# Retention kernel: first tables and products reordered at the head (broadcast table loads, a second DMA queue, twelve zero products)

## The chip, the cores and the metric

The kernel runs on one core of a Trainium2 chip, as one program and one launch. The metric is the device time of that core in microseconds, lower is better. The kernel before took 921.67 us (median of 3 runs, 921.03 to 922.06).

## The reference

Three layers follow one another. The first is a retention (attention with a decaying state) over 4 batches, 8 heads, 768 tokens, head size 64. The second and third are dense layers over the 3072 tokens.

```
state = gamma * state + k_t (outer) v_t          # per head, gamma = 1 - 2^(-5-h)
y_t   = (1/8) * q_t @ state
x     = y as (3072, 512)
h     = x @ w_in                                 # 512 -> 2048
g     = h if h >= 1, 0 if h <= -1, (h+1)^2/4 between
x     = g @ w_out                                # 2048 -> 512
then: softmax-gated layer of 1024, layer norm, times g_ln, @ w2_out
```

## The kernel before, in words

The retention is cut into 24 units: 4 batches of 6 chunks of 128 tokens. One unit `attention(u, env)` is a Python generator; it takes its queries and keys as a tile `qk` and its keys and values as a tile `kv` (512 KB each). The steps of a unit are these:

- Load `qk` (L183) and `kv` (L186) through SyncE's DMA queue, called SP below. Two yields follow.
- Scores `qp` on TensorE (L206): 8 products of 64 rows, two heads to each of four pairs.
- On VectorE `qn` = queries times the table `qdec` (L209, not for the first chunk of a batch). On GpSimd (POOL in the profile) keys times `vdec` (L211). On VectorE `sm` = scores times the table `dmat` (L215), once for each of the two head parities `o`. A yield follows.
- On TensorE `pv` = state times `qn` (L264, not for the first chunk) plus values times `sm` (L268), and `sp` = keys (decayed) times values (L273), which is what the chunk adds to the state.
- The result is split into a high and a low part (L104 on ScalarE, called ACT below, and L105 on VectorE, called DVE). The state is decayed (L280) and added to (L284, L286).

The tables are made by `tables()` (L298 to L309), called once after the first attention slot: `vdec` is loaded (L299), then `dmat` by four loads of 64 partitions each (L302), `gdec` (L303) and `qdec` (L304). Then for each `o` VectorE multiplies `dmat` by `vdec` (L306) and GpSimd sets what lies above the diagonal to zero (L307). GpSimd multiplies `qdec` by `gdec` (L309). In the source table of `dmat` the rows 0 to 63 are equal among each other, and so are the rows 64 to 127.

The order of work is set by a dictionary `sched` of slots: a unit is advanced by one yield in each of four slots. Unit 0 is advanced in the slots -11, -6, -5 and -4, unit 1 one slot later each, and so on. Weights of the second layer are loaded 512 KB at a time through the same SP queue (`load_w`, L113) seven or eight slots ahead and converted on ScalarE and VectorE (`conv_w`, L122 to L133). The first conversion step is the ACT instruction of L122. Within one engine the framework's planner orders the instructions by priority in a simulated timeline, then the order is fixed. `in_row()` adds dependencies that keep TensorE's instructions of a group in the order in which they were written.

At the start 40 products of zeros (`wps`, L413, 128x128 bf16) run on TensorE while the first loads are on their way. The dense layers (L363, L391, L493, L545) follow from about 45 us on.

Of the kernel before, what the change touches and what calls it, by code (L numbers as in the profile page):

```python
# [9 lines left out]
F32 = mybir.dt.float32  # L10
# [12 lines left out]
C = 128  # L23
NCH = S // C
NU = B * NCH
NPAIR = H // 2
# [12 lines left out]
ROW = CPB  # L39
W0 = -4  # L40
WARM = 40
PER = 4
GB = 3
HP_ATT = 1000
# [6 lines left out]
def kernel(  # L51
# [15 lines left out]
    nc = tc.nc  # L67
    ve, sc, gp, pe = nc.vector, nc.scalar, nc.gpsimd, nc.tensor
# [6 lines left out]
    ps_h = ctx.enter_context(tc.tile_pool(name="ps_h", bufs=2, space=bass.MemoryType.PSUM))  # L75
# [6 lines left out]
    vdec = const.tile([128, H, 1], F32, tag="vdec", name="vdec")  # L82
    gdec = const.tile([128, NPAIR, 1], F32, tag="gdec", name="gdec")
# [6 lines left out]
    @contextmanager  # L90
    def in_row():

        done, last = {i.name for i in nc.cur_bb.bb.instructions}, None
        yield
        for i in nc.cur_bb.bb.instructions:
            if i.name in done or i.engine != mybir.EngineType.PE:
                continue
            if last is not None:
                tc.add_manual_dep(i, last.name, mybir.DependencyInfo(
                    mybir.DependencyClass.NoSync, mybir.DependencyReason.DATA), reason="in a row")  # L100
            last = i
# [9 lines left out]
    def load_w(src, pool=wp):  # L111
        raw = pool.tile([128, 512, 2], U32, tag="w", name="w_raw")
        state["last_w"] = nc.sync.dma_start(raw.rearrange("p a t -> p (a t)"), src.bitcast(U32))  # L113
        return raw

    def conv_w(raw, scale=None):
        lw, hw = raw[:, :, 0], raw[:, :, 1]
        m = cv.tile([128, 512], F32, tag="wm", name="wm", bufs=3)
        p = cv.tile([128, 512], F32, tag="wp", name="wp", bufs=2)
        mu, mi = m.bitcast(U32), m.bitcast(I32)  # L120

        sc.activation(m, hw.bitcast(F32), AF.Abs)  # L122
        ve.tensor_scalar(m, m, W_MIN, W_MAX, op0=ALU.max, op1=ALU.min)

        sc.activation(p, lw, AF.Copy, bias=2.0, scale=2.0 ** -51)
        ve.tensor_scalar(mu, mu, 3, None, op0=ALU.logical_shift_left)
        ve.scalar_tensor_tensor(mu, hw, 0x80000000, mu, op0=ALU.bitwise_and, op1=ALU.bitwise_xor)  # L127
        ve.tensor_tensor(out=mi, in0=mi, in1=p.bitcast(I32), op=ALU.add)
        w = wp.tile([128, 2, 512], F32R, tag="w", name="w")
        hi, lo = w[:, 0, :], w[:, 1, :]  # L130
        if scale is None:
            sc.activation(hi, m, AF.Copy)
            ve.tensor_tensor(out=lo, in0=m, in1=fl(hi), op=ALU.subtract)  # L133
        else:
            sc.activation(hi, m, AF.Copy, scale=scale)
            ve.scalar_tensor_tensor(lo, m, scale, fl(hi), op0=ALU.mult, op1=ALU.subtract)
        return hi, lo
# [11 lines left out]
    def load_swapped(dst, src):  # L149
        n = NPAIR // 2  # L150
        ax = (slice(None),) * (len(dst.shape) - 3)
        nc.sync.dma_start(dst[(slice(None), *ax, slice(0, n))], src[(slice(None), *ax, slice(0, n))])
        for h in range(2):
            nc.sync.dma_start(dst[(slice(64 * h, 64 * h + 64), *ax, slice(n, 2 * n))],
                              src[(slice(64 - 64 * h, 128 - 64 * h), *ax, slice(n, 2 * n))])

    def attention(u, env):
# [4 lines left out]
        if blk == 0:  # L162
            def banks(*names):
                return [ps_acc.tile([128, 512], F32, tag="acc", name=n) for n in names]
# [16 lines left out]
        with (ExitStack() if early else tc.issue_after(state["last_w"].ins)):  # L181
            if not quad:
                nc.sync.dma_start(qk, qk_t[b, c])  # L183
            else:
                load_swapped(qk, qk_t[b, c])
            nc.sync.dma_start(kv, kv_t[b, c])  # L186
        yield
        yield
# [10 lines left out]
                sc.activation(env["dmat"][r][:, :2], dmat[:, r, :2], AF.Copy)  # L199
                sc.activation(env["dmat"][r][:, 2:], dmat[:, 1 - r, 2:], AF.Copy)  # L200
        qp = [t.rearrange("a (p c) -> a p c", p=NPAIR) for t in banks("qp0", "qp1")]
        with (in_row() if u >= ROW else ExitStack()):
            for p in range(NPAIR):
                for o in range(2):
                    r = slice(64 * o, 64 * o + 64)
                    pe.matmul(qp[o][:, p, :], qk[r, 1, p, :], qk[r, 0, p, :], start=True, stop=True)  # L206
        if not first:
            qn = attp.tile([128, NPAIR, C], F32, tag="qn", name="qn", bufs=1)
            ve.tensor_tensor(out=qn, in0=qk[:, 0], in1=env["qdec"], op=ALU.mult)  # L209
# [13 lines left out]
        if quad:  # L223
# [3 lines left out]
            with (in_row() if u >= ROW else ExitStack()):  # L227
                if not first:
                    for j in range(2):
                        for g in range(2):  # L230
                            for r in range(2):
                                o = r ^ g
                                pe.matmul(pv[r][64 * o:64 * o + 64, j, :], st[64 * r:64 * r + 64, 2 * g + j, :D],  # L233
                                          qn[64 * r:64 * r + 64, 2 * g + j, :], start=(j == 0), stop=False, skip_group_check=True)
                for r in (1, 0):
                    for j in range(2):
                        for o in range(2):
                            p = 2 * (r ^ o) + j
                            pe.matmul(pv[r][64 * o:64 * o + 64, j, :], kv[:, 1, 2 * p + o, :], sm[r][:, p, :],  # L239
                                      start=(first and j == 0), stop=(j == 1), skip_group_check=True)  # L240
                if not last:
                    for p in range(NPAIR):
                        for r in range(2):
                            h = 2 * p + (r ^ (p // 2))
                            pe.matmul(sp[64 * r:64 * r + 64, p, :], kv[:, 0, h, :], kv[:, 1, h, :],  # L245
                                      start=True, stop=True, skip_group_check=True)
# [14 lines left out]
        with (in_row() if u >= ROW else ExitStack()):  # L261
            if not first:
                for p in range(NPAIR):
                    pe.matmul(pv[:, p, :], st[:, p, :], qn[:, p, :],  # L264
                              start=(p == 0), stop=False, skip_group_check=True)
            for p in range(NPAIR):
                for o in range(2):
                    pe.matmul(pv[64 * o:64 * o + 64, p, :], kv[:, 1, 2 * p + o, :], sm[o][:, p, :],  # L268
                              start=(first and p == 0), stop=(p == NPAIR - 1), skip_group_check=True)
            if not last:  # L270
                for p in range(NPAIR):
                    for o in range(2):
                        pe.matmul(sp[64 * o:64 * o + 64, p, :], kv[:, 0, 2 * p + o, :], kv[:, 1, 2 * p + o, :],  # L273
                                  start=True, stop=True)
# [20 lines left out]
    dmat = attp.tile([128, 2, NPAIR, C], F32, tag="dmat", name="dmat", bufs=1)  # L295
    qdec = attp.tile([128, NPAIR, C], F32, tag="qdec", name="qdec", bufs=1)

    def tables():  # L298
        nc.sync.dma_start(vdec, vdec_d)  # L299
        for o in range(2):  # L300
            for dup in range(2):
                nc.sync.dma_start(dmat[64 * dup:64 * dup + 64, o], xtab_d[64 * o:64 * o + 64])  # L302
        nc.sync.dma_start(gdec, gdec_d)  # L303
        nc.sync.dma_start(qdec, xtab_d)  # L304
        for o in range(2):
            ve.tensor_tensor(out=dmat[:, o], in0=dmat[:, o], in1=vdec[:, o::2].to_broadcast([128, NPAIR, C]), op=ALU.mult)  # L306
            gp.affine_select(out=dmat[:, o], in_=dmat[:, o], pattern=[[0, NPAIR], [1, C]], compare_op=ALU.is_ge,  # L307
                             fill=0.0, base=0, channel_multiplier=-1)
        gp.tensor_tensor(out=qdec, in0=qdec, in1=gdec.to_broadcast([128, NPAIR, C]), op=ALU.mult)  # L309
# [17 lines left out]
    for u in range(NU):  # L327
        blk, k = divmod(u, CPB)
        x = (k - CPB, SA - CPB + k)[blk] if blk < 2 else base[blk] - NF + PER * k + 2
        at = (x - STEP0, x - 2, x - 1, x) if u < NWP else (x - 6, x - 3, x - 2, x)  # L330
        for n in at:
            sched.setdefault(n, []).append(u)
    gens = {}

    def att_slot(s):
        for u in sched.get(s, []):
            if u not in gens:
                gens[u] = attention(u, env)
            with (tc.high_priority(offset=HP_ATT) if u >= NWP else ExitStack()):
                next(gens[u], None)  # L340
# [3 lines left out]
    def weights_slot(s):  # L344
        for f in range(NF):
            at = max(first_use[f], W0 + 2 * f)
            if s == at - LD - 1:
                wraw[f] = [load_w(w_in[f])]
            if s == at - LD:
                wraw[f].append(load_w(w_out[f]))  # L350
            if s == at - CL:
                wi[f] = conv_w(wraw[f][0])
            if s == at - CL + 1:
                wo[f] = conv_w(wraw[f][1])
# [52 lines left out]

    if WARM:
        wz = const.tile([128, 128], mybir.dt.bfloat16, tag="wz", name="wz")
        ve.memset(wz, 0.0)  # L410
        wps = ps_h.tile([128, 512], F32, tag="h", name="wps")
        for n in range(WARM):
            pe.matmul(wps[:, :128], wz, wz, start=(n == 0), stop=(n == WARM - 1))  # L413
    for s in range(min(min(sched), -LD - 1), 0):
        att_slot(s)
        if s == min(sched):
            tables()
        weights_slot(s)

    w2 = [(w2_in[k, n], (k, n), w2i, None) for k in range(KD) for n in range(2)] + \  # L420
# [38 lines left out]
    if True:  # L459
# [94 lines left out]
        for t in range(NTILE + 3):  # L554
            if t % TPB == 0 and t // TPB + 1 < NBLK:
                load_x2(t // TPB + 1)
            for st in steps:
                n = int(st[-1]) if st[-1] in "01" and st[:2] in ("tr", "ou") else 2 if st == "out2" else 0
# [68 lines left out]
```

## Time and profile before

| what | value |
|---|---|
| median of 3 runs | 921.67 us (921.03 to 922.06) |
| the profiled execution | 921.52 us, its span on the core 919.7 us |
| TensorE busy | 902.7 us (98% of the span) |
| VectorE busy | 581.2 us (63%) |
| ScalarE busy | 406.2 us (44%) |
| GpSimd busy | 29.0 us (3%) |
| mean granted TensorE clock | 0.998 of full speed |
| moved by DMA | 75.35 MB, mean 82 GB/s |

The span goes from the first to the last instruction, and the execution's own time is 1.8 us longer. In the profile PE is TensorE, PEld its weight loads, DVE VectorE, ACT ScalarE, POOL GpSimd and SP SyncE. Times are in microseconds from the start of the span.

### The profile page before, as it was taken

What the parts mean: (1) busy time and instruction counts of PE and PEld (TensorE: products, weight loads), DVE (VectorE), ACT (ScalarE), POOL (GpSimd) and SP (SyncE); (2) the same over time, 40 slices, a digit from 0 to 9 for tenths busy, and PEclk for the clock granted to TensorE, in tenths of its full rate; (3) what the DMA queues carried; (4) which work ended last, traced back from release to release, by engine and by line L of the source; (5) the groups of instructions that cost most, each with busy time, mean ns of one, the idle gap of its engine ahead of it and who ended that gap; (6) DMA issues with size and microseconds to landing.
All of it is one profiled execution on the core that took longest, in us unless ns stands there. A gap on an engine that the chain in (4) does not pass through costs nothing.

```text
span 919.7 us, 12967 instructions
## 1 busy us (share of the span) xinstructions
PE 902.7 (98%) x5016; PEld 742.3 (81%) x5016; DVE 581.2 (63%) x1358; ACT 406.2 (44%) x765; POOL 29.0 (3%) x29
## 2 busy tenths in 40 slices
PE   8899999999999999999999999999999999999998
PEld 7678888887778887888888888888888888888886
DVE  5999997234354334332445449823988888888885
ACT  3768876333243444343445448732333333333322
POOL 3100100000010000000000000000000000000000
PEclk9999999999999999999999999999999999999999
DMA  9940821004431202220204114301111010100000
GB/s 338 407 160 24 321 70 58 1 23 138 126 127 47 69 24 93 69 62 8 75 18 148 59 37 148 118 0 47 47 60 43 29 63 24 69 24 24 24 24 34
DMA packets 30604, 75.35 MB, mean 82 GB/s; under 512 B 3920, under 2 KB 10448, under 8 KB 29776
## 3 DMA queue, kind: packets, MB, share of 16 engines
q1 hardware_dynamic: 29392, 72.44, 22.0%
q10 hardware_dynamic: 1152, 2.10, 1.0%
q8 instruction: 39, 0.64, 0.3%
q14 instruction: 21, 0.17, 0.1%
HBM read 59.85 MB, written 14.68 MB: 81 GB/s over the span
## 4 chain that ended last, share of the span: by engine, by line
PE 93%; DVE 2%; DMA 2%; ACT 1%; issue 0%; SPq 0%; ACTq 0%; DVEq 0%
PE acc L391 28%; PE hp L363 27%; PE h2p L493 14%; PE op L545 14%; PE tp L534 2%; PE pa L206 2%; PE pa L239 1%; DMA xs<-x2p 1%; PE pa L268 1%; PE pa L233 1%; PE qp L206 1%; PE pv L268 1%; PE pa L264 1%; DMA x2d<-xs 0%; PE pa L245 0%
## 5 line engine op out<-in xcount | busy, mean ns | idle before, releaser
L391 PE MATMUL acc<-gh,w 128*128 128x512 f32 x768 | 200.0, 392 | 4.0 <-DVE xs L404 2.4
L363 PE MATMUL hp<-xh,w 128*128 128x512 f32 x768 | 194.2, 392 | 1.6 <-ACT xh L104 1.4
L391 PEld LDWEIGHTS acc<-gh,w 128*128 128x128 f32 x768 | 142.9, 188 | 36.9 <-DVE xs L404 3.9
L363 PEld LDWEIGHTS hp<-xh,w 128*128 128x128 f32 x768 | 142.9, 188 | 33.1 <-ACT xh L104 1.9
L371 DVE SCALAR_TENSOR_TENSOR cs<-cs,hp 128x512 f32<-128x512 f32 x96 | 65.8, 685 | 150.9 <-ACT cs L370 150.4
L369 ACT ACTIVATE cs<-hp,half 128x512 f32<-128x512 f32 x96 | 66.0, 688 | 176.0 <-PE hp L363 164.7
L391 PE MATMUL acc<-gl,w 128*128 128x512 f32 x384 | 111.1, 393 | 0.0
L363 PE MATMUL hp<-xl,w 128*128 128x512 f32 x384 | 103.2, 390 | 0.0
L493 PE MATMUL h2p<-w,x2h 128*128 128x512 f32 x384 | 97.1, 395 | 0.0
L545 PE MATMUL op<-w,lh 128*128 128x512 f32 x384 | 91.4, 390 | 0.2 <-ACT lh L104 0.2
L105 DVE TENSOR_TENSOR gl<-cs,gh 128x512 fp32r<-128x512 f32 x96 | 67.2, 700 | 36.6 <-ACT gh L104 36.5
L545 PEld LDWEIGHTS op<-w,lh 128*128 128x128 f32 x384 | 71.9, 188 | 15.4 <-ACT lh L104 0.5
L363 PEld LDWEIGHTS hp<-xl,w 128*128 128x128 f32 x384 | 71.9, 188 | 15.3
L391 PEld LDWEIGHTS acc<-gl,w 128*128 128x128 f32 x384 | 71.4, 188 | 15.4 <-DVE wm L127 0.2
L493 PEld LDWEIGHTS h2p<-w,x2h 128*128 128x128 f32 x384 | 70.5, 188 | 13.7
L104 ACT ACTIVATE gh<-cs 128x512 fp32r<-128x512 f32 x96 | 60.4, 629 | 44.0 <-DVE cs L371 43.2
L370 ACT ACTIVATE cs<-cs 128x512 f32<-128x512 f32 x96 | 60.5, 630 | 3.9 <-DMA xs<-x2p 1.6
L503 ACT ACTIVATE e<-h2p,st 128x512 f32<-128x512 f32 x48 | 32.6, 685 | 60.1 <-DVE st L501 44.9
L493 PE MATMUL h2p<-w,x2l 128*128 128x512 f32 x192 | 51.6, 390 | 0.0
L104 ACT ACTIVATE x2h<-x2r 128x512 fp32r<-128x512 f32 x24 | 15.1, 631 | 76.2 <-PE h2p L493 58.6
L545 PE MATMUL op<-w,ll 128*128 128x512 f32 x192 | 47.7, 390 | 0.0
L500 DVE TENSOR_REDUCE st<-h2p 128x1 f32<-128x512 f32 x48 | 32.0, 688 | 18.4 <-PE h2p L493 18.3
(91 smaller groups left out, 996.2 us busy)
## 6 DMA issues: line engine op xcount, KB each, us to landing
kv<-in_kv_t_dram SPq DMA_DIRECT2D x24, 512.0 KB, 4.0
w_raw<-in_w_in_dram SPq DMA_DIRECT2D x24, 512.0 KB, 9.0
w_raw<-in_w_out_dram SPq DMA_DIRECT2D x24, 512.0 KB, 7.8
qk<-in_qk_t_dram SPq DMA_DIRECT2D x12, 512.0 KB, 7.9
x2d<-xs SPq DMA_DIRECT2D x24, 256.0 KB, 2.5
x2r<-x2d SPq DMA_DIRECT2D x6, 1024.0 KB, 4.8
out_dram<-o SPq DMA_DIRECT2D x24, 256.0 KB, 2.0
qk<-in_qk_t_dram SPq DMA_DIRECT2D x12, 256.0 KB, 3.4
```

The source lines that it names most:

```text
L104: sc.activation(hi, src, AF.Copy)
L105: ve.tensor_tensor(out=lo, in0=src, in1=fl(hi), op=ALU.subtract)
L206: pe.matmul(qp[o][:, p, :], qk[r, 1, p, :], qk[r, 0, p, :], start=True, stop=True)
L363: pe.matmul(hp, l[:, k * 128:(k + 1) * 128], r[:, k, :], start=(n == 0), stop=(n == 3 * KD - 1))
L369: sc.activation(cs, hp, AF.Relu, bias=half, scale=0.5)
L370: sc.activation(cs, cs, AF.Square)
L371: ve.scalar_tensor_tensor(cs, cs, 1.0, hp, op0=ALU.min, op1=ALU.max)
L391: pe.matmul(acc[d][:, :BLK], l[:, d * 128:(d + 1) * 128], r, start=(first and m == 1), stop=(last and m == 3))
L493: pe.matmul(hps[n], l[:, k, :], w2i[k, n][part], start=(m == 0), stop=(m == 3 * KD - 1))
L500: ve.tensor_reduce(st[:, n:n + 1], hps[n], axis=AX.X, op=ALU.max)
L503: sc.activation(e[:, n, :], hps[n], AF.Exp, bias=st[:, 2:3], accum_out=st[:, 3 + n:4 + n])
L545: pe.matmul(op, l[:, f, :], w2o[f][part], start=(n == 0), stop=(n == 3 * NF2 - 1))
```

## The change

Unit 0 gets one more yield, between the load of `qk` and the load of `kv`, and is advanced once right after `tables()`, so that its `kv` load stands behind the tables in SP's queue. `vdec` and `gdec` are loaded through ScalarE's DMA queue. `dmat` is loaded by two transfers, each of which reads one row of 2 KB of the source and writes it to all 128 partitions, in place of four transfers of 64 partitions each. Behind the scores of unit 0 stand 12 products of zeros (128 columns, bf16) into a PSUM tile that nothing reads, and scores and zeros of unit 0 are held in one row.

```diff
+FILL = 12
@@ attention()
             else:
                 load_swapped(qk, qk_t[b, c])
+            if u == 0:
+                yield
             nc.sync.dma_start(kv, kv_t[b, c])
         yield
         yield
@@
-        with (in_row() if u >= ROW else ExitStack()):
+        with (in_row() if u >= ROW or u == 0 else ExitStack()):
             for p in range(NPAIR):
                 for o in range(2):
                     r = slice(64 * o, 64 * o + 64)
                     pe.matmul(qp[o][:, p, :], qk[r, 1, p, :], qk[r, 0, p, :], start=True, stop=True)
+            if u == 0:
+
+                fill = ps_h.tile([128, 512], F32, tag="h", name="fill")
+                for n in range(FILL):
+                    pe.matmul(fill[:, :128], wz, wz, start=(n == 0), stop=(n == FILL - 1))
@@ tables()
-        nc.sync.dma_start(vdec, vdec_d)
+        nc.scalar.dma_start(vdec, vdec_d)
         for o in range(2):
-            for dup in range(2):
-                nc.sync.dma_start(dmat[64 * dup:64 * dup + 64, o], xtab_d[64 * o:64 * o + 64])
-        nc.sync.dma_start(gdec, gdec_d)
+            nc.sync.dma_start(dmat[:, o], xtab_d[64 * o:64 * o + 1].to_broadcast([128, NPAIR, C]))
+        nc.scalar.dma_start(gdec, gdec_d)
         nc.sync.dma_start(qdec, xtab_d)
@@ the first slots
         if s == min(sched):
             tables()
+            next(gens[0])
         weights_slot(s)
```

## Rows read from the trace of the kernel before

**Rows 1.** Busy time by stretch: start:end, length, then each engine's busy time (instructions).
```profile
core 0: us, PE busy (x) PEld busy (x) DVE busy (x) ACT busy (x) POOL busy (x), PEclk, DMA share, GB/s
0.00:24.00 24.00, 19.81 (x216) 17.88 (x216) 13.72 (x25) 8.15 (x17) 7.18 (x12) 0.93 0.93 341
24.00:45.00 21.00, 17.32 (x150) 13.27 (x149) 20.85 (x40) 14.28 (x29) 4.42 (x3) 1.00 1.03 406
45.00:919.70 874.70, 865.53 (x4652) 711.14 (x4652) 546.63 (x1296) 383.80 (x721) 17.37 (x14) 1.00 0.20 67
```

**Rows 2.** The chain that ended last, in order of time: start, length, what.
```profile
4.05 4.08 DMA dmat<-in_xtab_dram
...
9.17 0.69 DVE sm L215
...
9.91 0.38 PE pv L268
...
12.92 1.09 PE qp L206 x16
14.01 1.09 PE pv L264 x8
15.10 0.62 PE sp L273 x16
15.71 0.21 PE pv L268 x2
...
17.01 1.02 PE pv L268 x14
```

**Rows 3.** The same view as group 1, by single microseconds (seventh value: the granted clock).
```profile
9.00:10.00 1.00, 0.09 (x2) 0.10 (x4) 0.86 (x3) 0.00 (x0) 0.68 (x2) 0.64 1.10 369
10.00:11.00 1.00, 1.00 (x16) 1.00 (x18) 0.68 (x2) 0.00 (x0) 0.96 (x1) 0.50 0.95 352
...
12.00:13.00 1.00, 1.00 (x11) 0.76 (x9) 0.44 (x2) 0.05 (x1) 0.59 (x1) 0.65 1.00 389
```

**Rows 4.** Timeline of SP's queue: start of the issue, its length, line, transfer.
```profile
0.80 0.39 SPq L183 DMA_DIRECT2D qk<-in_qk_t_dram  x1
1.25 0.42 SPq L186 DMA_DIRECT2D kv<-in_kv_t_dram  x1
...
2.19 2.46 SPq L302 DMA_DIRECT2D dmat<-in_xtab_dram  x4
...
5.32 0.43 SPq L304 DMA_DIRECT2D qdec<-in_xtab_dram  x1
6.01 0.33 SPq L183 DMA_DIRECT2D qk<-in_qk_t_dram  x1
...
8.88 0.53 SPq L113 DMA_DIRECT2D w_raw<-in_w_in_dram  x1
```

**Rows 5.** DMA issues at those starts: size, us from issue to landing (vdec's issue: 1.72).
```profile
qk<-in_qk_t_dram SPq DMA_DIRECT2D x1, 512.0 KB, 3.7
kv<-in_kv_t_dram SPq DMA_DIRECT2D x1, 512.0 KB, 4.7
vdec<-in_vdec_dram SPq DMA_DIRECT2D x1, 4.0 KB, 4.5
qdec<-in_xtab_dram SPq DMA_DIRECT2D x1, 256.0 KB, 3.7
qk<-in_qk_t_dram SPq DMA_DIRECT2D x1, 512.0 KB, 4.3
w_raw<-in_w_in_dram SPq DMA_DIRECT2D x1, 512.0 KB, 10.3
```

**Rows 6.** Timeline of the compute engines: start, length, engine, line, instruction, idle before.
```profile
0.80 1.28 ACT L104 ACT_TABLE_LOAD   x1 [0.80 <-PEq L613]
1.08 4.45 PE L413 MATMUL wps<-wz 128*128 128x128 bf16 x40 [1.08 <-DVE wz L410]
5.46 1.34 PE L206 MATMUL qp<-qk 64*128 64x128 f32 x16
8.07 0.64 POOL L307 TENSOR_SCALAR_AFFINE_SELECT dmat<-dmat 128x512 f32<-128x512 f32 x1 [0.64 <-DVE dmat L306]
12.41 1.04 POOL L211 TENSOR_TENSOR kv<-kv,vdec 128x512 f32<-128x512 f32 x1 [1.45 <-DMA kv<-in_kv_t_dram]
20.75 0.66 ACT L122 ACTIVATE wm<-w_raw 128x512 f32<-128x512 f32 x1
```

## The prediction, made before the changed kernel ran

> **What bounds the kernel now.** I first split the span into three stretches [rows 1]. From 45 us on TensorE is busy 865.5 of 874.7 us: nothing in this change touches that part, it can only start earlier or later. From 24 to 45 us VectorE is busy 20.85 of 21.00 us: converting weights bounds it, so this part too only moves as a block, if its inputs move with it. What is open is the head, where TensorE lacks 4.2 of 24 us and the clock averages 0.93. The chain of waits tells what the head hangs on [rows 2]: the decay table `dmat`, issued last at 4.05 us and landed at 8.13, then a VectorE product, then `sm` at 9.17, and unit 0's `pv` at 9.91. From there to 24 us TensorE has work without a gap. TensorE had finished the scores at 6.80 [rows 6], so it stood still for 3.1 us. In that gap the granted clock fell, between 9 and 10 us; it was 0.50 from 10 to 11, which is the 1.2 GHz level, and came back to 2.4 GHz between 12 and 13 [rows 3]. The price is readable: unit 0's `pv` and `sp` took 9.91 to 12.92, so 3.01 us. Unit 1's same products took 0.62 + 0.21 + 1.02 = 1.85 us [rows 2]. So the cold clock costs 1.16 us.
>
> **The transfers.** In SP's queue transfers land in order. `qk` of unit 0 lands at 0.80 + 3.7 = 4.50, `kv` at 1.25 + 4.7 = 5.95, `qdec` at 5.32 + 3.7 = 9.02, unit 1's `qk` at 6.01 + 4.3 = 10.31 [rows 4, 5]. The last step is 512 KB in 1.29 us, or 406 GB/s, the rate of the whole stretch after 24 us [rows 1]. A table half of 256 KB over 128 partitions is thus worth between 0.64 us (half of 1.29) and 0.89 us (`qdec`'s 9.02 less `dmat`'s 8.13, with `gdec` in between). I take 0.75, nearer the first, as `gdec` no longer stands in this queue. Reading one row 128 times has no row in this trace; it is a rival below.
>
> New landings: `dmat` halves 5.25 and 6.00, `qdec` 6.75, `kv` of unit 0 at 8.04, unit 1's `qk` at 9.33, so 0.98 us sooner than before (0.56 at 0.89 a piece). The issue does not limit: `kv` is the fifth, so issued by about 3 us, against 4.65 us before for the end of `dmat`'s four alone [rows 4]. So `dmat` comes 2.1 us sooner and `kv` 2.1 us later; unit 0 needs both.
>
> **The small tables on ScalarE's queue.** `vdec` took 4.5 us to land [rows 5]. ScalarE has nothing but a table load of 1.28 us at 0.80 until 12.95 us [rows 6]. If the issue stands ahead of that load, `vdec` lands at 5.3, if behind, at 6.6. I take 6.0, the middle, as no row decides. Nothing else on ScalarE waits behind these two issues.
>
> **Unit 0 after.** VectorE's two products with `vdec` take about 0.69 us each, the length of `sm` on the same shape [rows 2]: 6.0 to 7.4. GpSimd's two selects of 0.64 us [rows 6] end at 7.4 and 8.1. `sm` runs 7.4 to 8.1 and 8.1 to 8.8; its scores are done at 6.80. The first `pv` product can start at 8.1, when `kv` has just landed, and half of `pv` has to wait for the second `sm`. GpSimd still has two jobs of 1.04 us [rows 6]: keys times `vdec` (`kv` at 8.04) and `qdec` times `gdec`. If the keys go first, `sp` starts at 9.2 and the products, 1.85 us warm, end at about 10.2; unit 1's scores (1.09) follow, and its state product at 11.3, against 14.01 before: 2.7 us gained. If `qdec` goes first, `sp` starts at 10.2, its 0.62 us and the state copy (two halves, about 0.9) follow, and the state product is at 11.8: 2.2 us gained. I take 2.5. Of this 1.2 is the clock and 1.3 the earlier `pv`.
>
> **The zeros.** Forty of them took 4.45 us [rows 6], 0.11 us each. Twelve are 1.3 us at that pace and, an estimate, 0.67 at twice the pace. The scores stand at 1.34 us for 16 against 1.09 for unit 1 [rows 2, 6], so TensorE is then near its full pace: the zeros run 6.8 to 7.5, or to 8.1 at worst, before `pv` can start. They cost nothing in TensorE's queue as long as `kv` lands at 8.0. Should it land sooner than 7.5, they would cost at most what is left of them. They leave a gap of at most 0.8 us, where the clock fell no sooner than 9.0, 2.2 us after the last score product. The `in_row` only pins the order that this row already shows.
>
> **What is late next.** Unit 1's `sp` needs its `kv`, which landed at 12.41, plus 1.04 on GpSimd [rows 6], and it ran at 15.10: 1.65 us of slack. It comes about 1 us sooner at least, so it asks for at most 0.1 of the 2.7. The next late thing is the first weight tile: landed 8.88 + 10.3 = 19.18 [rows 4, 5], first used by ScalarE at 20.75 [rows 6], slack 1.57 us. The use can come at most 1.57 + 0.98 = 2.55 us sooner, or 1.57 + 0.56 = 2.13 with the slower transfers. So 2.5 us nearly fits; I take off 0.15. All later steps, the block from 24 to 45 us and everything behind it, move as they are.
>
> **Sum.** 2.5 - 0.15 = 2.35 us. The profiled execution took 921.52 us, span 919.7; it becomes 919.17. The median shown is 0.15 above it, so 919.3.
>
> **Rivals.**
> 1. *The weights hold it back.* If the queue runs no sooner than before (two small tables and the new loads take as long as the old set), the first weight lands at 19.18 still, and the gain ends at its slack of 1.57 us: 920.1. For it speaks that all bytes are still moved, that the DMA share is 0.93 over the head, and that this is the tightest slack. Against it, four half-width transfers took 8.13 - 5.95 = 2.18 us (with `vdec`) where two take about 1.5. Chance 0.2, with the halved rate below.
> 2. *The zeros do not hold the clock.* The change then does not do what it says there: unit 0's products start at 8.3 but take 3.01 us, to 11.3 in place of 12.92: 1.6 us, 920.1. For it speaks that 12 zeros are short beside the 3.1 us gap. Against it stand the 2.2 us for which the clock held. Chance 0.1.
> 3. *The spread reads collide.* All 128 reads of a half aim at one row of 2 KB, where before every partition read its own. If they serialise, both halves come late, and `qdec`, `kv`, unit 1 and the weights stand behind them in SP's queue. With the second half at T, `kv` comes at T + 2.04; the gap on TensorE is then as long as before, so the products take 3.01 us and end at T + 5.05. That is the old 12.92 when T is 7.87, so 1.7 us a half, 156 GB/s: below this rate the change loses. At a quarter of 406 GB/s (each half 2.58 us) T is 9.66, and unit 0 ends at 14.7: 1.8 us slower, 923.5. For it speaks that no transfer in this trace reads so; against it, that the sixteen engines move 406 GB/s from rows of different addresses with no sign of a bound at the source. Chance 0.12.
>
> At half rate (1.29 us a half) T is 7.07, `kv` lands at 9.1, unit 1's `qk` at 10.4, and the weights' slack leaves 1.5 us of gain: 920.2, counted with rival 1. The Trainium skill, "DMA: Bandwidth & Descriptors", section "Latency and other measured facts", speaks against the change here: streams whose rows lie so that all partitions hit the same memory channel fell to about half of the full rate (its example: 207 to 103 GB/s), by an inferred mechanism. By that page the sum would be 920.2. No run here shows it yet.
>
> **How the numbers follow.** The forecast has 0.58: 917.7 (2.7 us of head, unit 1's `kv` catching up as well, and up to 1 us from a planner that sets the conversions in another order) to 919.8. Rivals 1 and 2 have 0.30 near 920.1; rival 3 has 0.12. A measurement of this kernel tells a difference from 0.2%, 1.84 us, so below 919.83 is faster: 0.58 faster, 0.30 the same, 0.12 slower. The range runs from 917.7 to 922.0: it takes in rivals 1 and 2 and the mild end of 3, and leaves out the rest of it and an unexpected loss or gain of order in the VectorE stretch.
>
> **What would show it.** Right: `dmat` landing near 6.0, `pv` of unit 0 at 8.1 to 8.8, a granted clock of 1.00 from 9 to 13 us, unit 1's state product at 11.3 to 11.8, and VectorE's full stretch starting 2.3 us sooner. Wrong: `dmat` halves that land more than 1 us apart (rival 3); ScalarE's first conversion waiting for a weight DMA (rival 1); 0.50 in the clock after 9 us (rival 2); or a head that is 2.4 us shorter and a stretch from 24 to 45 us that is longer, which would mean that the planner's new order took it back.

## The result, and the profile after

| what | before | after |
|---|---|---|
| median | 921.87 us (921.03 to 924.01, 4 runs) | 932.74 us (932.07 to 933.23, 4 runs) |
| ratio | | 1.01, 95% interval [1.0085, 1.0116] |
| the profiled execution, its span | 921.52, 919.7 us | 933.23, 931.1 us |
| TensorE busy | 902.7 us | 906.7 us |

The changed kernel is about 1% slower; the forecast was 0.26% faster. The profiled spans differ by 11.4 us. TensorE's idle time (span less busy time) grew from 17.0 to 24.4 us, so 7.4 us. Its busy time grew by 4.0 us: 0.8 of it is the twelve new products of zeros, the rest goes with stretches at a lower clock. Where each of the two arose is read from the stretches.

**The head.** The timeline of SP's queue after the change, and then single microseconds (columns as in [rows 1], the clock seventh):

```profile
1.25 0.90 SPq L309 DMA_DIRECT2D dmat<-in_xtab_dram  x2
2.18 0.43 SPq L311 DMA_DIRECT2D qdec<-in_xtab_dram  x1
2.66 0.43 SPq L189 DMA_DIRECT2D kv<-in_kv_t_dram  x1
```
```profile
5.00:6.00 1.00, 1.00 (x17) 0.90 (x17) 0.19 (x1) 0.00 (x0) 0.00 (x0) 1.00 0.94 99
6.00:7.00 1.00, 1.00 (x20) 0.88 (x17) 0.51 (x1) 0.00 (x0) 0.42 (x1) 1.00 0.86 193
7.00:8.00 1.00, 0.20 (x4) 0.02 (x1) 0.00 (x0) 0.00 (x0) 0.22 (x1) 1.00 1.05 395
...
11.00:12.00 1.00, 0.84 (x14) 0.84 (x16) 0.83 (x2) 0.00 (x0) 0.39 (x1) 0.91 1.03 422
12.00:13.00 1.00, 1.00 (x19) 1.00 (x16) 0.00 (x0) 0.42 (x1) 0.45 (x1) 0.50 1.03 414
```

The issues are as early as forecast. But while `dmat` is read, the rate falls to 99 GB/s, and the second half lands at 8.0 us. Timelines of TensorE, VectorE and GpSimd in that head (columns as in [rows 6]):

```profile
5.26 1.16 PE L209 MATMUL qp<-qk 64*128 64x128 f32 x16
6.36 0.84 PE L214 MATMUL fill<-wz 128*128 128x128 bf16 x12
10.04 0.40 PE L276 MATMUL pv<-sm,kv 128*64 128x128 f32 x2 [2.84 <-DMA kv<-in_kv_t_dram]
11.16 1.17 PE L276 MATMUL pv<-sm,kv 128*64 128x128 f32 x13 [0.71 <-DVE sm L223]
...
13.32 2.06 PE L209 MATMUL qp<-qk 64*128 64x128 f32 x16
15.31 1.16 PE L272 MATMUL pv<-qn,state 128*128 128x128 f32 x8
```
```profile
5.81 0.69 DVE L313 TENSOR_TENSOR dmat<-dmat,vdec 128x512 f32<-128x512 f32 x1 [4.79 <-DMA dmat<-in_xtab_dram]
8.02 0.69 DVE L313 TENSOR_TENSOR dmat<-dmat,vdec 128x512 f32<-128x512 f32 x1 [1.52 <-DMA dmat<-in_xtab_dram]
...
10.41 0.69 DVE L223 TENSOR_TENSOR sm<-qp,dmat 128x512 f32<-128x512 f32 x1 [1.10 <-POOL dmat L314]
```
```profile
6.58 0.63 POOL L314 TENSOR_SCALAR_AFFINE_SELECT dmat<-dmat 128x512 f32<-128x512 f32 x1 [5.27 <-DVE dmat L313]
8.76 1.04 POOL L316 TENSOR_TENSOR qdec<-qdec,gdec 128x512 f32<-128x512 f32 x1 [1.54 <-DMA qdec<-in_xtab_dram]
9.75 0.64 POOL L314 TENSOR_SCALAR_AFFINE_SELECT dmat<-dmat 128x512 f32<-128x512 f32 x1
```

TensorE waits 2.84 us for `kv` after the zeros end at 7.20, and the clock is at 0.50 from 12 to 15 us. Then it waits 0.71 us for the second `sm`, because GpSimd did the queries' table (L316) between the two selects (L314). Unit 1's state product (L272, the measure of the head from here on) starts at 15.31. In the same view of the kernel before it starts at 13.94 (14.01 in the chain of [rows 2]):

```profile
13.94 1.16 PE L264 MATMUL pv<-qn,state 128*128 128x128 f32 x8
```

That is 1.4 us of the 11.4.

**Behind the head.** The products of the second layer start at 27.7 us in the kernel before, among the units of the retention, and not only at about 45. A product of `x` with `w_in` is called `hp` (L370 in the changed kernel). Its activation takes the steps `cs` (two on ScalarE, one on VectorE), and the result is split into `gh` and `gl`. These are multiplied by `w_out` into the accumulators `acc` (L398), which are copied out as `xs`. Three stretches, first of the kernel before, then of the changed one with a row for 24 to 45 us ahead (columns as in [rows 1]):

```profile
46.60:70.00 23.40, 23.27 (x162) 18.20 (x162) 23.32 (x45) 15.09 (x26) 0.00 (x0) 1.00 0.38 147
70.00:90.00 20.00, 20.00 (x116) 16.22 (x116) 18.00 (x34) 16.77 (x33) 0.00 (x0) 1.00 0.04 14
90.00:110.00 20.00, 20.00 (x90) 16.51 (x88) 19.54 (x38) 16.59 (x29) 4.13 (x2) 1.00 0.94 346
```
```profile
24.00:45.00 21.00, 18.51 (x164) 14.57 (x160) 20.81 (x39) 14.97 (x30) 5.93 (x3) 1.00 1.03 406
...
46.60:70.00 23.40, 22.88 (x146) 17.70 (x146) 23.36 (x46) 16.30 (x28) 0.00 (x0) 1.00 0.46 172
70.00:90.00 20.00, 17.45 (x116) 14.07 (x114) 19.85 (x39) 14.32 (x28) 0.00 (x0) 1.00 0.00 1
90.00:110.00 20.00, 15.43 (x66) 12.34 (x67) 18.98 (x34) 15.89 (x29) 1.79 (x2) 0.83 0.74 251
```

Between 46.6 and 110 us TensorE lost 0.39 + 2.55 + 4.57 = 7.5 us of busy time. VectorE was the fuller engine there: 19.85 of 20 us from 70 to 90, where it had 18.00 before. TensorE's waits in these stretches are new; the largest, and its place in the timelines of TensorE, ScalarE and VectorE:

```profile
PE hp L370 <- DVE cs L378: 4.7, 1, 4.7
```
```profile
89.45 0.39 PE L398 MATMUL acc<-gl,w 128*128 128x512 f32 x1
94.57 3.78 PE L370 MATMUL hp<-xh,w 128*128 128x512 f32 x8 [4.74 <-DVE cs L378]
98.15 1.91 PE L370 MATMUL hp<-xl,w 128*128 128x512 f32 x4
...
101.11 1.98 PE L370 MATMUL hp<-xh,w 128*128 128x512 f32 x8
102.93 1.07 PE L370 MATMUL hp<-xl,w 128*128 128x512 f32 x4
```
```profile
90.34 0.67 ACT L376 ACTIVATE cs<-hp,half 128x512 f32<-128x512 f32 x1
90.91 0.66 ACT L123 ACTIVATE wm<-w_raw 128x512 f32<-128x512 f32 x1
...
92.60 0.62 ACT L377 ACTIVATE cs<-cs 128x512 f32<-128x512 f32 x1
```
```profile
93.23 0.69 DVE L128 SCALAR_TENSOR_TENSOR wm<-w_raw,wm 128x512 uint32<-128x512 uint32 x1
93.84 0.68 DVE L378 SCALAR_TENSOR_TENSOR cs<-cs,hp 128x512 f32<-128x512 f32 x1
```

The activation of a finished product stands in the engines' fixed orders among conversions of weights (`wm`, `w`). TensorE idles, then the clock drops: the twelve `hp` products from 94.57 us take 3.78 and 1.91 us, the next twelve from 101.11 us 1.98 and 1.07, so some 2.6 us more. With the 7.5 and the head's 1.4 that makes 11.5; behind 110 us TensorE idles some half a microsecond less. So the head explains little more than a tenth of the 11.4.

The traces also hold the orders themselves. By line and tile, VectorE's instructions stand in another order than before from the 9th to the 252nd of 1358, the last of them at 151 us. ScalarE's differ up to 150 us too, TensorE's up to 121 us, and a few loads and stores of SP's queue between 86 and 95 us. Behind that the orders are the same.

### The profile page after: what moved, and what is told of

Read it like the earlier page. It is cut to its first block, busy times and chain, and to the rows that moved or that the text cites. A ratio compares the mean times of both kernels' runs of the same rounds, so it can differ in the third digit from the quotient of the medians.

```text
span 931.1 us, 12979 instructions
## 1 busy us (share of the span) xinstructions
PE 906.7 (97%) x5028; PEld 745.4 (80%) x5028; DVE 582.7 (63%) x1358; ACT 406.4 (44%) x765; POOL 29.2 (3%) x29
## 4 chain that ended last, share of the span: by engine, by line
PE 87%; DVE 6%; DMA 6%; issue 1%; ACT 0%; SPq 0%; DVEq 0%; ACTq 0%
PE acc L398 26%; PE hp L370 25%; PE h2p L501 14%; PE op L553 14%; PE tp L542 2%; PE pa L209 2%; DMA xs<-x2p 2%; DMA w_raw<-in_w_in_dram 1%; PE pa L247 1%; DVE wm L128 1%; DVE wm L129 1%; DMA qk<-in_qk_t_dram 1%; DMA kv<-in_kv_t_dram 1%; DVE w L134 1%; DMA w_raw<-in_w_out_dram 1%; PE pa L241 1%
## 5 line engine op out<-in xcount | busy, mean ns | idle before, releaser
L370 PE MATMUL hp<-xh,w 128*128 128x512 f32 x768 | 196.0, 395 | 9.5 <-DVE cs L378 4.7
L398 PE MATMUL acc<-gh,w 128*128 128x512 f32 x768 | 200.0, 393 | 2.2 <-DVE xs L411 2.1
L370 PEld LDWEIGHTS hp<-xh,w 128*128 128x128 f32 x768 | 144.0, 189 | 41.6 <-DVE cs L378 5.2
L398 PEld LDWEIGHTS acc<-gh,w 128*128 128x128 f32 x768 | 143.3, 188 | 34.8 <-DVE xs L411 3.2
L378 DVE SCALAR_TENSOR_TENSOR cs<-cs,hp 128x512 f32<-128x512 f32 x96 | 65.8, 686 | 157.0 <-ACT cs L377 156.5
L398 PE MATMUL acc<-gl,w 128*128 128x512 f32 x384 | 110.5, 392 | 0.0
L370 PE MATMUL hp<-xl,w 128*128 128x512 f32 x384 | 104.2, 393 | 0.5 <-DVE xl L106 0.5
L370 PEld LDWEIGHTS hp<-xl,w 128*128 128x128 f32 x384 | 72.4, 189 | 16.3 <-DVE xl L106 0.9
L398 PEld LDWEIGHTS acc<-gl,w 128*128 128x128 f32 x384 | 71.6, 188 | 15.3 <-DVE wm L129 0.2
```

Of the source, the lines that this page charges most:

```text
L370: pe.matmul(hp, l[:, k * 128:(k + 1) * 128], r[:, k, :], start=(n == 0), stop=(n == 3 * KD - 1))
L378: ve.scalar_tensor_tensor(cs, cs, 1.0, hp, op0=ALU.min, op1=ALU.max)
L398: pe.matmul(acc[d][:, :BLK], l[:, d * 128:(d + 1) * 128], r, start=(first and m == 1), stop=(last and m == 3))
```

## The experiments

Where an order is held, a list of positions per engine was added and each instruction was tied to the one before it in the list without a semaphore; nothing else is changed (abridged, the lists left out):

```diff
+    rows = {DVE: [...], Activation: [...], PE: [...], SP: [...]}
+    for engine, row in rows.items():
+        seen = [i for i in instructions if i.engine == engine]
+        for a, b in zip(row, row[1:]):
+            tc.add_manual_dep(seen[b], seen[a].name, NoSync)
```

**1. Is it the head or the order behind it?** The whole change with the order of before held behind unit 0, and the kernel before with the changed kernel's order held there.

> The whole change, but behind unit 0 the instructions of TensorE, VectorE, ScalarE and SP's queue are held in the order that the kernel before had; nothing is left out. Theory A (the planner's new order behind the head costs most of the 11 us): only the head's loss stays, unit 1's state product at 15.3 against 14.0, so 1.4 to 2 us over before, 923.3 to 924. Rival B (the late and cold head makes everything behind it late, whatever the order): about 932, as the changed kernel.

> The kernel before with its own head (loads, tables, unit 0), and behind it the order that the changed kernel had; nothing is left out. Theory A: the order alone costs 11 less the head's 1.4 to 2, so 930 to 931. Rival B: 922, as the kernel before.

Measured: the change with the old order 923.66 us (10 runs, before 923.11 beside it), ratio 1.0009 [0.9996, 1.0023]; the old head with the new order 931.77 us, 1.0093 [1.0062, 1.0124]. In the traces the first differs from before in the order of unit 0's own products and of two steps of VectorE, and nowhere behind; VectorE's, ScalarE's and TensorE's orders in the second are the changed kernel's but for the same rows. GpSimd's was not held; it differs in the head alone. The order alone makes nearly all of the loss. From 70 to 110 us the first (two rows) is as full as before; the second (two rows) is not:

```profile
70.00:90.00 20.00, 20.00 (x116) 16.30 (x115) 17.95 (x35) 16.04 (x31) 0.00 (x0) 1.00 0.04 14
90.00:110.00 20.00, 20.00 (x90) 16.54 (x89) 19.55 (x37) 16.07 (x29) 2.56 (x2) 1.00 0.82 306
```
```profile
70.00:90.00 20.00, 17.61 (x111) 14.35 (x110) 19.81 (x40) 13.64 (x27) 0.00 (x0) 0.91 0.00 1
90.00:110.00 20.00, 16.88 (x78) 13.26 (x77) 18.77 (x34) 16.32 (x30) 1.04 (x1) 0.91 0.70 236
```

**2. Is reading one row 128 times slow?** The change with a table that is stored as 128 rows, each with an address of its own, and the kernel before with the two one-row loads alone.

```diff
-            nc.sync.dma_start(dmat[:, o], xtab_d[64 * o:64 * o + 1].to_broadcast([128, NPAIR, C]))
+            nc.sync.dma_start(dmat[:, o], dtab_d[:, o])
```

> The changed kernel with its own order, but each half of the decay table is read from 128 separate rows of a larger table, in place of one row read 128 times. Theory A: the halves land at about 5.3 and 6.0 in place of 5.8 and 8.0, the head gains 2 to 3.5 us and the order keeps its cost: 929 to 931. Rival B: the head is repaired and with it everything: 919 to 922. If one row is not slower to read than 128 rows (rival C): the halves land as before, 932.

> The kernel before, with only the decay table's four loads replaced by two that read one row 128 times each; the order of all instructions stays that of before. The reads of one row are slow (2.2 us a half in the changed kernel, against 1.0 here for a half of two pieces): the second half lands at 10.5 in place of 8.1, so 2 to 3 us slower, 924 to 925, by theory A. Rival B: the delay grows behind the head as in the changed kernel, 930 or more. Rival C (one row is as fast): the halves land at 7.6 or sooner, 0.5 us faster.

Measured: with 128 rows 932.2 us, ratio 1.0081 [1.0055, 1.0108]; one row in the kernel before 924.09 us, 1.001 [0.9993, 1.0027]. The same bytes and the same number of transfers; single microseconds of the first and of the second kernel:

```profile
5.00:6.00 1.00, 1.00 (x17) 0.90 (x16) 0.01 (x1) 0.00 (x0) 0.00 (x0) 1.00 1.04 394
6.00:7.00 1.00, 0.87 (x14) 0.67 (x12) 1.00 (x2) 0.00 (x0) 0.24 (x1) 1.00 1.07 416
```
```profile
6.00:7.00 1.00, 0.74 (x14) 0.54 (x10) 0.00 (x0) 0.00 (x0) 0.91 (x1) 1.00 0.79 78
7.00:8.00 1.00, 0.00 (x0) 0.00 (x0) 0.00 (x0) 0.00 (x0) 0.14 (x1) 1.00 0.80 144
```

With distinct rows the halves land at 5.85 and about 6.5 us, and unit 1's state product starts at 14.04 in place of 15.31. The read of one row is slow, and it costs the head 1.3 us. I had expected 2 to 3.5 us there; with distinct rows TensorE still waits for GpSimd's second select. Under the new order, which this run keeps by line and tile, the total does not follow: 932.2. In the kernel before the order stays the old one, and the halves land at 7.9 and 9.7 (10.5 was expected for the second).

**3. What is the head worth under the old order?** The change with 128 rows and the old order; then also with GpSimd's order set to select, select, keys, queries' table (and VectorE's copy of the state ahead of `qn`).

> The changed kernel with the decay table read from 128 separate rows, and behind unit 0 the order of the kernel before. Theory A: the head of the run with 128 rows in its own order (unit 1's state product at 14.0, as before) and no loss behind it: ratio to before 0.999 to 1.000. If the 128 rows alone were of use only in the new order, 1.001 as with the one row in the old order.

> As the run with 128 rows and the old order, and GpSimd's first jobs in the order select, select, keys, queries' table, where the planner put the queries' table between the two selects; on VectorE the state copy stands ahead of qn. The second half of the table is then ready at about 8.0 in place of 9.4, pv of unit 0 starts at about 8.2 and the state product of unit 1 at about 11.7 with the clock up: 2 us faster than before, ratio 0.9975 to 0.9985. If the first weights hold it back, 0.9985 to 0.9995.

Measured: 921.26 us, ratio 0.9983 [0.9971, 0.9995], and 920.6 us (12 runs, before 922.85 beside it), 0.9974 [0.9964, 0.9984]. The second beats both kernels. In it TensorE's timeline is

```profile
8.57 1.51 PE L277 MATMUL pv<-sm,kv 128*64 128x128 f32 x15 [1.63 <-DVE sm L224]
...
10.59 1.16 PE L210 MATMUL qp<-qk 64*128 64x128 f32 x16
12.80 1.13 PE L273 MATMUL pv<-qn,state 128*128 128x128 f32 x8 [1.05 <-DVE qn L218]
```
```profile
11.59 1.07 DVE L218 TENSOR_TENSOR qn<-qk,qdec 128x512 f32<-128x512 f32 x1
```

with a granted clock of 1.00 over the whole head. The second fence is VectorE's step on which the state product waits.

**4. What do the zeros do?** The changed kernel without them (the planner's orders stay the same by line and tile), and the best version without them.

```diff
-                fill = ps_h.tile([128, 512], F32, tag="h", name="fill")
-                for n in range(FILL):
-                    pe.matmul(fill[:, :128], wz, wz, start=(n == 0), stop=(n == FILL - 1))
```

> The changed kernel in its own order without the twelve products of zeros (scores of unit 0 no longer held in a row). The changed kernel lost the clock at about 11.9 us although it had the zeros, so they hold nothing there: ratio to before as the changed kernel, 1.009 to 1.011. If they do put the loss of the clock off, it falls at about 9.5 us and comes back sooner or costs up to 1 us more: 1.010 to 1.012.

> The version with 128 rows for the table, the order of before behind unit 0 and GpSimd's keys ahead of its queries' table, without the twelve products of zeros. If the zeros hold the clock there, it falls to 0.50 after 8 us without them and unit 0's products take about 3 us in place of 1.9, so the state product of unit 1 comes 1 to 1.2 us later than 12.80 and the time is 921.3 to 922.0 against 920.6 with zeros. If the gap is by now too short for the clock to fall, the clock stays at 1.00 and the time is 920.4 to 920.8, the same.

Measured: 934.83 us, ratio 1.013 [1.0111, 1.015], against the changed kernel's 1.01; and 921.65 us, 0.9982 [0.997, 0.9993], against 0.9974 with zeros. Both pairs of intervals overlap, so no effect on the time is settled. (1.013 lies above the range expected; 921.65 lies where I had put the time for a fallen clock, though the clock held.) The clock tells more: without zeros the first stands at 0.50 from 9 us (first fence), the second, where TensorE waits 1.48 us, at 1.00 (second):

```profile
9.00:10.00 1.00, 0.00 (x0) 0.00 (x0) 0.45 (x1) 0.00 (x0) 1.00 (x2) 0.50 1.01 414
```
```profile
9.00:10.00 1.00, 0.90 (x18) 0.90 (x19) 0.04 (x1) 0.00 (x0) 1.00 (x2) 1.00 1.01 414
```

So in the changed kernel, with 2.84 us to wait, the zeros put the fall off (to 12 us); in the best version the wait is short, and the clock holds without them.

**5. Is it one misplaced step of the new order?** In the changed kernel's order, two products' activation steps were moved ahead of the conversion steps of VectorE and ScalarE among which they had stood; then the four copies out of the accumulators too. The lists in short, not as code (`+` inserted, `-` taken out; the second run's `xs` moves in double signs):

```diff
 DVE: ... [+cs, cs, gl, gl+] [++xs, xs++] w(L134) ... [-cs, cs, gl, gl-] [--xs, xs--]
 ACT: ... [+cs, cs, cs, cs, gh, gh+] [++xs, xs++] w(L133) ... [-cs, ..., gh-] [--xs, xs--]
```

> The changed kernel in its own order, except that the activation steps of two hidden products (cs: two steps on ScalarE and one on VectorE each, and the split that follows) stand ahead of three or four weight conversions, where the planner had put them behind. If the new order costs what it costs because a product's activation waits behind conversions that nothing needs yet, TensorE's 4.7 us wait at 89.8 us shrinks to under 1 us and its slow clock after it (94.6 to 99.8 us, about 2.6 us) goes: 4 to 7 us faster than the changed kernel, ratio to before 1.003 to 1.006. If the loss is spread over the whole order, or the conversions were needed, the ratio stays at 1.008 to 1.010.

> The changed kernel's order once more, with the two products' activation steps as in the run before it, and now also the four copies out of the accumulators (two on VectorE, two on ScalarE) moved ahead of the five weight conversions. Theory A (the loss is work for TensorE that stands behind conversions on VectorE and ScalarE, and these six steps are it): the 4.7 us and 2.7 us waits of TensorE both go, the clock stays at 1.00 from 90 to 110 us, and 4 to 6 us come back: 927 to 929. Theory B (the order as a whole has too few finished weights and activations at the right time, so a mended place only shifts the stall): 931 to 934 again, with a new wait of TensorE of 2 us or more between 90 and 110 us.

Measured: 933.17 us, ratio 1.0104 [1.0088, 1.012], and 934.78 us, 1.0121 [1.0096, 1.0147]. No gain in either; my expectation of one for the first missed. The 4.7 us wait goes or shrinks, and others come. Waits of TensorE from 80 to 125 us in the first and in the second:

```profile
PE acc L398 <- ACT w L133: 2.7, 1, 2.7
```
```profile
PE hp L370 <- DVE cs L378: 2.7, 1, 2.7
...
PE pa L209 <- DMA qk<-in_qk_t_dram: 2.1, 1, 2.1
```

**6. Which part of the change turns the order over, and is another order as bad?** The one-row loads leave every engine's order behind the head as it was (experiment 2), and taking out the zeros does not change the new one (experiment 4). The small tables on ScalarE's queue alone, and unit 0's late `kv` alone, each give a new order, and not the same one.

```diff
-        nc.sync.dma_start(vdec, vdec_d)
+        nc.scalar.dma_start(vdec, vdec_d)
...
-        nc.sync.dma_start(gdec, gdec_d)
+        nc.scalar.dma_start(gdec, gdec_d)
```

> The kernel before with one part of the change alone: the two small tables through ScalarE's queue. The head hardly moves (the table lands up to 0.5 us sooner), but the planner gives a new order behind it. If any new order is worse than the one of before, it loses several us: 925 to 933. If the loss belongs to the changed kernel's order alone, it is 921.0 to 923.5.

```diff
+            if u == 0:
+                yield
             nc.sync.dma_start(kv, kv_t[b, c])
...
             tables()
+            next(gens[0])
```

> The kernel before with one part of the change alone: unit 0's keys and values loaded behind the tables. The table lands about 1.3 us sooner, the keys land near 9.3 us, so unit 0's products start at most 1 us sooner. If any new order behind the head is worse, 925 to 933; if the loss belongs to the changed kernel's order alone, 921.0 to 923.5, and if the head's gain stays as well, 920.5 to 921.5.

Measured: the small tables alone 941.13 us (before 923.25 beside it), ratio 1.0187 [1.0154, 1.0219]; the late `kv` alone 929.71 us, 1.0066 [1.0042, 1.0091]. Both lose, in different places; the first lies above the 925 to 933 us that I had expected. The late `kv` has its gap from 70 to 90 us (first row). With the small tables the clock is at 0.50 until 29 us although TensorE is recorded as busy throughout. In its order there unit 1's scores, too, are split around the products of the unit before (the kernel before does so from unit 2 on). ScalarE's first conversion starts at 29.38 in place of 20.75 [rows 6], 8.6 us of the 22.7 by which that profiled span is longer (the last two fences):

```profile
70.00:90.00 20.00, 15.80 (x108) 12.67 (x107) 19.52 (x39) 15.78 (x30) 0.00 (x0) 1.00 0.00 1
```
```profile
12.00:16.00 4.00, 4.00 (x24) 3.44 (x24) 1.64 (x4) 0.31 (x1) 1.92 (x2) 0.50 1.04 412
...
29.00:30.00 1.00, 1.00 (x18) 1.00 (x18) 0.69 (x1) 0.97 (x4) 0.00 (x0) 0.59 1.01 402
```
```profile
29.38 0.66 ACT L122 ACTIVATE wm<-w_raw 128x512 f32<-128x512 f32 x1
```

Side by side, with the start of unit 1's state product as the measure of the head:

| order behind unit 0 | kernel | state product at | ratio to before |
|---|---|---|---|
| of before | 128 rows, GpSimd's order set | 12.80 us | 0.9974 |
| of before | the same without zeros | 12.81 | 0.9982 |
| of before | the kernel before | 13.94 | 1 |
| of before | 128 rows | 14.27 | 0.9983 |
| of before | the change | 15.71 | 1.0009 |
| of before | before, one-row loads | 16.07 | 1.001 |
| of the change | 128 rows | 14.04 | 1.0081 |
| of the change | head of before (its clock was low from 8 us) | 15.10 | 1.0093 |
| of the change | the changed kernel | 15.31 | 1.01 |
| of the change | without zeros | 15.76 | 1.013 |
| another | late `kv` alone | 13.74 | 1.0066 |
| another | small tables alone | 17.58 | 1.0187 |

Each start is that of one profiled execution, and equal heads differ in it: 13.94 and 15.10 with the head of before, 15.31 to 16.17 with that of the change (the runs of experiments 1 and 5 among them). Within that spread the time follows the head under the old order: 3.3 us later there cost 0.36%, so 3.3 us. Under the new one every head costs 0.8 to 1.3%.

## Why the prediction was wrong

**The step that failed** is the one that priced everything behind the head at nothing: from 45 us on "nothing in this change touches that part, it can only start earlier or later", and "All later steps, the block from 24 to 45 us and everything behind it, move as they are." They do not, because the planner set VectorE, ScalarE, TensorE and some transfers of SP's queue in another order, up to some 150 us. Experiment 1 shows it from both sides: the same change under the old order is at 1.0009, the old head under the new order at 1.0093. The text allowed "up to 1 us from a planner that sets the conversions in another order", and only as a gain, and its range left an "unexpected loss or gain of order" out; the order measured 0.93%, so some 9 us of loss. (The lower bound is 0.3 us off its own sum, too: 2.7 and 1 us from 921.67 make 918.0, not 917.7. Nothing hangs on it here.) The sign "that would mean that the planner's new order took it back" was meant for 24 to 45 us. There VectorE is as full as before (20.81 against 20.85 of 21.00 us); the loss falls at 70 to 110, where [rows 1] had shown TensorE full and I took that for safe. A full TensorE there was the result of one order, not a property of the stage: VectorE was at 90 to 98% in the same stretch.

**Transfers.** The issue times were right. "I take 0.75" for a table half was wrong: forecast 5.25 and 6.00, measured 5.75 and 8.0, so about 2.3 us for the second half, some 115 GB/s. `kv` of unit 0 landed at 9.9 (forecast 8.04) and the first weight at 20.4 (forecast about a microsecond before 19.18). With distinct rows the halves were 0.67 us apart, so the size of the term was right for such rows. Their first half landed at 5.85, no sooner than that of one row: the second carried the delay.

**Rival 3 was true** as far as the head goes, at 0.12 of the chance: reading one row 128 times is slow. That the reads serialise, as it put it, is not shown beyond the rate. Its own formula fits: with T at 8.0 it gives `kv` at 10.04 and the products' end at 13.05; `pv` started at 10.04 and unit 1's scores at 13.32. That it comes so near is partly luck: the clock was up for the first 1.8 us of these products, and the 0.71 us of waiting for the second `sm`, which it does not have, stood in for that. What it left out is that these scores, too, ran at the low clock: 2.06 us against 1.09 [rows 2]. 0.40 and 0.97 make the 1.4 us. Yet the loss of rate is larger than the one that the Trainium skill gives for rows a large power of two apart ("DMA: Bandwidth & Descriptors", section "Latency and other measured facts": 207 to 103 GB/s, so about half): some 115 GB/s against 391 from distinct rows is less than a third. Whether it is the mechanism of that page no run here shows. Under the old order the slow read costs 1.0009 less 0.9983, so 0.26%.

**The zeros.** "They leave a gap of at most 0.8 us" failed with `kv`'s landing; the gap was 2.84 us. The clock held until 11 us and not through unit 0's products: rival 2 true in part. That twelve of them cost nothing was right; they ended at 7.20 (forecast 7.5).

**ScalarE's queue.** `vdec` landed at 0.79 + 3.7 = 4.5, sooner than the 6.0 I took; its issue stood ahead of the table load. In transfer time no cost of the move shows. In planning it was the dearest part tried alone.

**Unit 0 after.** The prediction let GpSimd's two selects follow one another; the planner put the queries' table between them, and the second `sm` came at 10.41. In the best version, where table, clock and order are as the prediction had them, `pv` starts at 8.57 (forecast 8.1) and the state product at 12.80 (forecast 11.3 to 11.8, before 13.94). What the forecast lacked is `qn`: it needs GpSimd's `qdec` times `gdec`, then VectorE 1.07 us behind the state copy, and TensorE waits 1.05 us for it. The head thus gains 1.1 us, not 2.5. The total gains 0.26% [0.16, 0.36], 2.4 us, though the profiled spans differ by 1.2 only (918.5 and 919.7); I leave that open within the interval.

**What stays open.** The new order as a whole is the cause; what makes it bad is not settled. It isn't the one place with the largest wait, nor that and the copies behind it: mending them moved the stall on (experiment 5). A reading that fits, but was only argued, is that in the new order finished conversions run ahead of the activations that TensorE needs, over tens of microseconds. The traces show that much: by 100 us VectorE has started 19 last steps of conversions (L134) and 8 of activations (L378), where before it had started 17 (L133) and 10 (L371). But in the mended orders it is 18 or 17 and still 8, so conversions that run ahead are not all of it. Which engine's order it is was not separated. Why the clock stayed low for 18 busy microseconds with the small tables alone is open too.

## What to carry to other kernels

Where a planner orders the instructions from a simulated timeline, moving a load or a yield can be an edit of everything planned after it: compare the orders first, hold the old one, and only then judge the edit. Five orders other than the one of before were timed here (three planned, two mended by hand), and all were 0.7 to 1.9% slower, while every version under the old order lay within 0.3% of before. A table that is spread to 128 partitions was better stored as 128 rows than read from one here (0.26% under the old order), and products of zeros are to be tried after the wait has been shortened: then the clock may hold by itself.

## What the runs showed of the hardware that was not expected

- Two transfers of 256 KB that each read one row of 2 KB 128 times landed 1.7 to 2.6 us apart in six runs (78 to 144 GB/s in the microseconds that they filled); from 128 distinct rows each, 0.67 us apart (394 to 416 GB/s).
- After twelve products of zeros and a wait of 2.84 us the clock still stood at 1.00 from 10 to 11 us, and fell only once the products had begun at 10.04 (0.91 from 11 to 12, 0.50 from 12 to 15). Without the zeros it stood at 0.50 from 9 us, ahead of products that began at 10.18.
- With the small tables alone the clock stood at 0.50 from 11 to 29 us with TensorE recorded as busy for all of it, and rose between 29 and 30 (0.59). In the kernel before it was back between 12 and 13 us, 3 us after the products began [rows 3].
